# Buffers of one SBUF and PSUM slot each, chosen by the kernel's own planner

## The chip, the core and the metric

The program runs on one core of a Trainium2 chip. The metric is the device time of one execution in microseconds (us); less is better. The core has a matrix engine (TensorE, PE in the profile, with its weight loads as PEld), a vector engine (DVE), a scalar engine (ACT), a general engine (POOL, hardly used here), and a sync engine (SP), whose queue issues every DMA of this kernel.

## The reference

Three layers follow each other: an attention over 32 memory slots for each of 8 batches and 8 heads (576 tokens each), then two feed-forward layers over the 4608 tokens, all in float32.

```python
a = softmax(phi)                                  # over the 32 slots
k_m, v_m = einsum('bhsm,bhsd->bhmd', a, k), einsum('bhsm,bhsd->bhmd', a, v)
attn = softmax(q @ k_m.T / sqrt(64));  x = attn @ v_m       # [4608, 512]
x = (s * relu(x @ w_in) ** 2 + b) @ w_out                   # 512 -> 2048 -> 512
x = gelu_sigmoid(x @ w1) @ w2                               # 512 -> 2048 -> 512
```

## The kernel before, in words

Each float32 operand of a large product is split into a high and a low part (`hi`, `lo`, with tiles named oh and ol, or ah and al, mh and ml for the first product), and each product is three matmuls: high by high, high by low, low by high. The second to fourth products are cut in 2 by 2 blocks and use seven block products in place of eight (three forms of Strassen's scheme), which is why blocks are subtracted from each other (`minus`, `half`) ahead of the split. Products accumulate in PSUM in tiles named X, Y and Z, and while one of them is being added up, its state is copied out several times (tiles a, u2, u4 and c12, called a, u and c in the profile).

The time falls in four stages. Until about 300 us runs the attention with the first product (its results h are rectified and stored to DRAM as r). Then `down("wo")` runs until about 650 us, `up` (to the tiles g, a and ab, stored to DRAM) until about 1000 us, and `last` until the end. Between stages the data goes through DRAM, so every stage loads its blocks by DMA (A, B, C, D, E, x) and stores its results by DMA. All of these share one in-order queue on SP.

The order of the work isn't written out by hand. The methods of `Net` hand operations to an `Order`: each has a due time, one or more engines with a cost, and the tiles that it reads and writes. `Order.sort` then plans: it goes through the operations that are ready, reckons for each when it could start (its engine's time, the ends of what it reads, and a slot for each new tile), and takes one after the other. The list that comes out is the order in which instructions are issued, engine by engine; nothing reorders an engine later.

Slots: `BUFS` gives the number of buffers of each tag: 31 of tag t (nearly every block, operand and result), 30 of tag w (weights), 4 of tag ps (PSUM), and a few small ones. The planner keeps a heap `free[tag]` of the reckoned times at which slots come free. An operation that makes a new tile starts no earlier than the smallest of them; when the operation is taken, that time is popped. When the last user of a tile has been planned, the reckoned end of its last use plus 0.2 us is pushed. A DMA's reckoned end is its start plus its KB over 340 plus 3.0 us. The heap holds times alone, so the planner doesn't say which slot a tile gets.

That is settled by the framework. `Net.t` asks a pool for a tile with `tag=k[0]` and `bufs=` the number of `BUFS`. The framework gives the new tile one of the tag's slots and makes the first instruction that writes it wait until every instruction that used the slot's former tile has ended. If that is on another engine or a DMA, the wait is a semaphore wait, and what is queued behind the waiting instruction on its engine waits as well.

Lines of the profile that the prediction uses: L1049 to L1051 are the matmuls of `up` into X or Y, L1118 to L1120 those into Z in `phase`, L1182 to L1184 those of `last` and L1284 to L1286 its Z; L1061 is ScalarE's copy of X into u2 or u4, L266 and L267 the high part, L272 a subtraction, the low part or an addition on VectorE, L815 the rectified h, L261 the DMA. The planner's own lines in the diff are in `Order.sort`, and the pool's call is in `Net.t`.

Of the kernel before, what the change touches and what calls it, by code (L numbers as in the profile page):

```python
# [27 lines left out]
class Order:  # L28
# [14 lines left out]
    def __init__(self, bufs):  # L43
        self.bufs, self.ops, self.rank, self.fill, self.until, self.since = bufs, [], [], None, 0, 0
        self.narrow = set()
        self.wrote, self.read, self.users = {}, {}, {}

    def add(self, due, ways, r=(), w=(), first=0):
# [19 lines left out]
    def sort(self):  # L68
        ops, rank = self.ops, self.rank
        left = [len(o[2]) for o in ops]  # L70
        after = [[] for _ in ops]
        tiles = {}
        for n, (due, _, deps, new) in enumerate(ops):
            for d in deps:
                after[d].append(n)
            for x in new:
                tiles.setdefault(x[0], []).append((due, n, x))
        queue = {tag: [x for _, _, x in sorted(v, key=lambda e: e[:2])] for tag, v in tiles.items()}
        free = {tag: [0.0] * n for tag, n in self.bufs.items()}
        uses = {x: len(v) for x, v in self.users.items()}  # L80
        last = dict.fromkeys(uses, 0.0)
        at, end, on, out = {}, [0.0] * len(ops), [None] * len(ops), []
        of = [[] for _ in ops]
        for x, v in self.users.items():
            for n in v:
                of[n].append(x)
        run = False
        held = {"dve": 0.0, "pool": 0.0}
        ready = sorted((rank[n], n) for n in range(len(ops)) if not left[n])
        since = {n: 0.0 for _, n in ready}  # L90
        while ready:
            can = {}
            limit = ready[0][0] + self.AHEAD
            for due, n in ready:
                if due > limit and can:
                    break
                _, ways, deps, new = ops[n]
                t0 = 0.0
                if new:
                    ok = True  # L100
                    for tag in {x[0] for x in new}:
                        mine = [x for x in new if x[0] == tag]
                        f = free[tag]
                        if len(f) < len(mine) or any(x not in queue[tag][:len(f)] for x in mine):
                            ok = False
                            break
                        t0 = max(t0, f[0] if len(mine) == 1 else heapq.nsmallest(len(mine), f)[-1])
                    if not ok:
                        continue
                best = None  # L110
                for i, (eng, cost, _, port) in enumerate(ways):
                    t = max(t0, at.get(eng, 0.0))
                    if port:
                        t = max(t, held["dve" if eng == "pool" else "pool"])
                    for d in deps:
                        e = end[d] + (self.LAG[eng] if on[d] != eng else 0.05)
                        if e > t:
                            t = e
                    score = t + cost * self.WEIGHT.get(eng, 1.0)
                    if best is None or score < best[0]:  # L120
                        best = score, t, eng, i
                can.setdefault(best[2], []).append((best[1], due, n, best[3]))
            if not can:
                raise RuntimeError("no order")
            first = []
            for tag, v in can.items():
                t0 = min(v)[0]
                like = [c for c in v if c[0] <= t0 + 0.1 and c[2] in self.narrow and c[1] >= self.since] if tag == "pe" and run else ()
                if like:
                    c = min(like, key=lambda c: c[1:])  # L130
                    if c[1] < min(v, key=lambda c: c[1:])[1] + self.NEAR:
                        first.append(c)
                        continue
                first.append(min((c for c in v if c[0] <= t0 + (self.SLACK if c[1] < self.until else 0.0)), key=lambda c: c[1:]))
            t, _, n, i = min(first)
            _, ways, _, new = ops[n]
            eng, cost, fn, port = ways[i]
            if port:
                held[eng] = t + cost
            if self.fill and eng == "pe":  # L140
                out.append(lambda n=int((t - at.get(eng, 0.0)) * self.FILL): self.fill and self.fill(n))
            for x in new:
                queue[x[0]].remove(x)
                heapq.heappop(free[x[0]])
            at[eng], on[n] = t + cost, eng
            end[n] = t + cost + (3.0 if eng == "sync" else 0.0)
            ready.remove((rank[n], n))
            if eng == "pe":
                run = n in self.narrow
            out.append(fn)  # L150
            for m in after[n]:
                left[m] -= 1
                if not left[m]:
                    bisect.insort(ready, (rank[m], m))
            for x in of[n]:
                last[x] = max(last[x], end[n])
                uses[x] -= 1
                if not uses[x]:
                    heapq.heappush(free[x[0]], last[x] + 0.2)
        self.span = max(end)  # L160
        self.end, self.on = end, on
        return out


class Net:
# [50 lines left out]
    def t(self, k, shape, dt=F32):  # L216

        self.n += 1
        pool = self.ps if k[0] == "ps" else self.sb
        x = pool.tile(shape, dt, tag=k[0], bufs=self.BUFS[k[0]], name=f"{self.name(k)}_{self.n}")  # L220
        self.T[k] = x
        return x

# [1255 lines left out]
```

## Time and profile before

| | us |
|---|---|
| median of 3 runs | 1352.02 (1351.92 to 1352.36) |
| the profiled execution, whole | 1353.97 |
| its span, from the first to the last instruction | 1352.2 |
| TensorE busy | 1335.0 |
| VectorE busy | 1103.3 |
| ScalarE busy | 843.2 |

The profiled execution's whole time is 1.8 us above its span and 1.95 us above the median of the runs that were timed without a profile. Matmuls overlap and their ends are modelled, so how often a matmul starts says more than the busy time does. The granted clock of TensorE was full (a mean of 0.997) except in the first slices of the span.

### The profile page before, as it was taken

The numbers are of one execution on the slowest core, as the hardware profiler recorded it, in microseconds if no ns is written. First come the engines' busy times: TensorE is split into PE (matmuls) and PEld (weight loads), VectorE is DVE, ScalarE is ACT, GpSimd is POOL, SyncE is SP. The second block draws the span as 40 slices with busy tenths as digits, with TensorE's granted clock in tenths as the row PEclk, the third lists the DMA queues.
The fourth block names the chain that finished last, engine by engine and source line by source line (L and its number), as shares of the span: only waits on it lengthen the run. The fifth ranks groups of instructions, "written<-read, shape, count | busy, mean of one in ns | idle before, by whom it ended". The sixth has DMA issues, their size and how long they took to land.

```text
span 1352.2 us, 24079 instructions
## 1 busy us (share of the span) xinstructions
PE 1335.0 (99%) x9112; PEld 1293.7 (96%) x9112; DVE 1103.3 (82%) x1568; ACT 843.2 (62%) x1164; POOL 52.2 (4%) x42
## 2 busy tenths in 40 slices
PE   6999999999999999999999999999999999999998
PEld 5888888899999999999999999999999999999998
DVE  6878996899998897999875778594376988889796
ACT  4766666788877887787654655564455454355452
POOL 2201220200000000000000000000000000000000
PEclk8999999999999999999999999999999999999999
DMA  9989999797755685499989699978998765747563
GB/s 364 352 299 353 361 344 329 259 325 261 280 190 168 221 318 164 180 318 332 375 326 369 243 340 333 319 263 302 382 333 305 242 207 180 257 140 240 173 207 121
DMA packets 141091, 374.37 MB, mean 277 GB/s; under 512 B 15920, under 2 KB 18480, under 8 KB 140976
## 3 DMA queue, kind: packets, MB, share of 16 engines
q1 hardware_dynamic: 140976, 372.85, 78.5%
q8 instruction: 71, 1.16, 0.4%
q14 instruction: 44, 0.36, 0.1%
HBM read 235.10 MB, written 137.69 MB: 276 GB/s over the span
## 4 chain that ended last, share of the span: by engine, by line
PE 92%; DVE 4%; DMA 3%; issue 0%; ACT 0%; SPq 0%; ACTq 0%
PE X L1184 5%; PE X L1183 5%; PE X L1182 5%; PE X L1049 5%; PE X L1051 5%; PE X L1050 5%; PE X L909 5%; PE X L911 5%; PE X L910 5%; PE h L296 4%; PE h L298 4%; PE h L297 4%; PE Y L910 2%; PE Y L1184 2%; PE Y L911 2%; PE Y L1182 2%
## 5 line engine op out<-in xcount | busy, mean ns | idle before, releaser
L296 PE MATMUL h<-ah,mh 128*128 128x288 f32 x512 | 155.1, 303 | 0.2
L298 PE MATMUL h<-ah,ml 128*128 128x288 f32 x512 | 151.3, 295 | 0.1
L297 PE MATMUL h<-al,mh 128*128 128x288 f32 x512 | 150.8, 295 | 0.0
L1049 PE MATMUL X<-oh,w 128*128 128x384 f32 x384 | 128.6, 335 | 1.1 <-ACT u L1061 1.1
L911 PE MATMUL X<-oh,wo 128*128 128x384 f32 x384 | 128.4, 334 | 0.0
L910 PE MATMUL X<-ol,wo 128*128 128x384 f32 x384 | 128.4, 334 | 0.0
L909 PE MATMUL X<-oh,wo 128*128 128x384 f32 x384 | 128.3, 334 | 0.0
L1050 PE MATMUL X<-ol,w 128*128 128x384 f32 x384 | 128.3, 334 | 0.0
L1051 PE MATMUL X<-oh,w 128*128 128x384 f32 x384 | 128.3, 334 | 0.0
L1183 PE MATMUL X<-ol,w 128*128 128x384 f32 x384 | 128.3, 334 | 0.0
L1182 PE MATMUL X<-oh,w 128*128 128x384 f32 x384 | 128.3, 334 | 0.0
L1184 PE MATMUL X<-oh,w 128*128 128x384 f32 x384 | 128.3, 334 | 0.0
L815 ACT ACTIVATE r<-h 128x576 f32<-128x576 f32 x126 | 88.7, 705 | 61.7 <-PE h L298 45.9
L296 PEld LDWEIGHTS h<-ah,mh 128*128 128x128 f32 x512 | 96.1, 188 | 13.7 <-issue 6.6
L272 DVE TENSOR_TENSOR u<-Y,u 128x768 f32<-128x768 f32 (+1 forms) x62 | 57.5, 928 | 51.4 <-PE Y L1051 34.1
L266 ACT CAST oh<-C 128x768 fp32r<-128x768 f32 x82 | 70.8, 872 | 45.4 <-PE X L910 11.6
L272 DVE TENSOR_TENSOR ol<-A,oh 128x768 fp32r<-128x768 f32 x96 | 88.7, 953 | 12.1 <-issue 3.7
L298 PEld LDWEIGHTS h<-ah,ml 128*128 128x128 f32 x512 | 96.1, 188 | 0.5 <-DVE ml L272 0.4
L297 PEld LDWEIGHTS h<-al,mh 128*128 128x128 f32 x512 | 96.2, 188 | 0.0
L272 DVE TENSOR_TENSOR ol<-C,oh 128x768 fp32r<-128x768 f32 x84 | 79.4, 955 | 17.9 <-PE X L911 3.4
L266 ACT CAST oh<-A 128x768 fp32r<-128x768 f32 x91 | 77.0, 867 | 16.8 <-DVE ol L272 5.1
L1049 PEld LDWEIGHTS X<-oh,w 128*128 128x128 f32 x384 | 72.1, 188 | 1.8 <-ACT u L1061 1.8
(269 smaller groups left out, 3710.5 us busy)
## 6 DMA issues: line engine op xcount, KB each, us to landing
w<-w SPq DMA_DIRECT2D x120, 512.0 KB, 6.2
r<-r SPq DMA_DIRECT2D x128, 288.0 KB, 4.3
kv<-in_kv SPq DMA_DIRECT2D x72, 258.0 KB, 5.1
g<-u SPq DMA_DIRECT2D x48, 384.0 KB, 4.5
raw<-in_w SPq DMA_DIRECT2D x32, 512.0 KB, 5.9
q<-in_q SPq DMA_DIRECT2D x32, 288.0 KB, 5.6
A<-r SPq DMA_DIRECT2D x24, 384.0 KB, 5.0
B<-r SPq DMA_DIRECT2D x24, 384.0 KB, 5.1
```

Of the source, the lines that this page charges most:

```text
L272: self.order.add(due, [self.dve(n, lambda: nc.vector.tensor_tensor(out(), a(), b(), op=op), port=port)], r, w, first)
L296: self.nc.tensor.matmul(ps, wh, xh, start=start and i == 0, stop=False)
L297: self.nc.tensor.matmul(ps, wh, xl, start=False, stop=False)
L298: self.nc.tensor.matmul(ps, wl, xh, start=False, stop=(i == n - 1))
L909: nc.tensor.matmul(out, T[w][:, 0, c], T[h][:, p], start=f, stop=False, skip_group_check=True)
L910: nc.tensor.matmul(out, T[w][:, 0, c], T[l][:, p], start=False, stop=False, skip_group_check=True)
L911: nc.tensor.matmul(out, T[w][:, 1, c], T[h][:, p], start=False, stop=last, skip_group_check=True)
L1049: nc.tensor.matmul(out, T[w][:, 0, c], T[h][:, k], start=f, stop=False, skip_group_check=True)
L1050: nc.tensor.matmul(out, T[w][:, 0, c], T[l][:, k], start=False, stop=False, skip_group_check=True)
L1051: nc.tensor.matmul(out, T[w][:, 1, c], T[h][:, k], start=False, stop=k == 1, skip_group_check=True)
L1182: nc.tensor.matmul(out, T[w][:, 0, c], T[h][:, p], start=f, stop=False, skip_group_check=True)
L1184: nc.tensor.matmul(out, T[w][:, 1, c], T[h][:, p], start=False, stop=last, skip_group_check=True)
```

## The change

The heap of free slots holds pairs of a reckoned time and a slot's number in place of times. The slot that is popped for a new tile is kept in `Order.slot`, and goes back to the heap with the reckoned time at which the tile's last use ends. `Net.t` asks the pool for a tile of a tag that has the slot's number in it (t0, t1, and so on), with one buffer. So the framework has nothing to choose: the tile waits for the former tile of that slot. The reckoned times are the same pairs' first parts, so the planned order of the operations, their engines and the number of slots stay as they were.

```diff
-        free = {tag: [0.0] * n for tag, n in self.bufs.items()}
+        free = {tag: [(0.0, i) for i in range(n)] for tag, n in self.bufs.items()}
...
-                        t0 = max(t0, f[0] if len(mine) == 1 else heapq.nsmallest(len(mine), f)[-1])
+                        t0 = max(t0, f[0][0] if len(mine) == 1 else heapq.nsmallest(len(mine), f)[-1][0])
...
             for x in new:
                 queue[x[0]].remove(x)
-                heapq.heappop(free[x[0]])
+                self.slot[x] = heapq.heappop(free[x[0]])[1]
...
                 if not uses[x]:
-                    heapq.heappush(free[x[0]], last[x] + 0.2)
+                    heapq.heappush(free[x[0]], (last[x] + 0.2, self.slot[x]))
...
-        x = pool.tile(shape, dt, tag=k[0], bufs=self.BUFS[k[0]], name=f"{self.name(k)}_{self.n}")
+        x = pool.tile(shape, dt, tag=f"{k[0]}{self.order.slot[k[:2]]}", bufs=1, name=f"{self.name(k)}_{self.n}")
```

## Rows read from the trace of the kernel before

**Rows 1.** The page, part 1: each engine's busy us, share, instructions.

```profile
PE 1335.0 (99%) x9112; PEld 1293.7 (96%) x9112; DVE 1103.3 (82%) x1568; ACT 843.2 (62%) x1164; POOL 52.2 (4%) x42
```

**Rows 2.** Windows: stretch, its length, each engine's busy us, clock, DMA share, GB/s.

```profile
0.00:62.00 62.00, 50.42 (x514) 41.59 (x522) 47.27 (x78) 37.11 (x61) 15.80 (x16) 0.94 0.96 358
62.00:300.00 238.00, 237.66 (x2550) 206.49 (x2535) 202.65 (x318) 164.49 (x247) 36.42 (x26) 1.00 0.93 324
300.00:650.00 350.00, 349.92 (x2041) 349.57 (x2040) 316.11 (x410) 281.73 (x383) 0.00 (x0) 1.00 0.73 248
650.00:1000.00 350.00, 348.86 (x2012) 348.17 (x2011) 241.84 (x394) 191.89 (x261) 0.00 (x0) 1.00 0.89 323
1000.00:1352.00 352.00, 348.19 (x2009) 347.87 (x2007) 295.44 (x371) 167.98 (x216) 0.00 (x0) 1.00 0.63 214
```

**Rows 3.** The chain that ended last, whole span: start us, us, what.

```profile
861.25 7.36 DMA g<-u
...
1348.23 0.56 DVE u L272
```

**Rows 4.** Waits of TensorE, whole span: us in total, times, longest us.

```profile
PE s L578 <- DMA kv<-in_kv: 4.6, 2, 3.0
...
PE X L1049 <- ACT u L1061: 1.1, 2, 0.7
```

**Rows 5.** Timeline, 868 to 870: start us, us, engine, line, what, idle before.

```profile
868.62 0.34 PE L1119 MATMUL Z<-ol,w 128*128 128x384 f32 x1
...
868.70 0.80 ACT L1061 COPY u<-X 128x768 f32<-128x768 f32 x1 [5.86 <-DMA g<-u]
868.79 0.34 PE L1120 MATMUL Z<-oh,w 128*128 128x384 f32 x1
869.16 0.33 SPq L261 DMA_DIRECT2D x<-x  x1
...
869.55 0.44 PE L1049 MATMUL X<-oh,w 128*128 128x384 f32 x1 [0.43 <-ACT u L1061]
```

**Rows 6.** Timeline, 975 to 986, of SP, TensorE and ScalarE.

```profile
975.27 0.32 SPq L261 DMA_DIRECT2D g<-ab  x1
...
981.81 0.33 PE L1051 MATMUL X<-oh,w 128*128 128x384 f32 x1
...
983.89 0.34 PE L1120 MATMUL Z<-oh,w 128*128 128x384 f32 x1
...
984.09 0.80 ACT L1061 COPY u<-X 128x768 f32<-128x768 f32 x1 [5.88 <-PE Z L1119]
984.26 0.79 SPq L261 DMA_DIRECT2D A<-g  x2
...
984.94 0.44 PE L1049 MATMUL X<-oh,w 128*128 128x384 f32 x1 [0.71 <-ACT u L1061]
```

**Rows 7.** DMAs of 968 to 986, and of the whole span: KB, us to landing.

```profile
g<-ab SPq DMA_DIRECT2D x1, 384.0 KB, 3.6
...
g<-u SPq DMA_DIRECT2D x48, 384.0 KB, 4.5
```

**Rows 8.** Timeline of TensorE, 75 to 77.

```profile
75.80 0.29 PE L297 MATMUL h<-al,mh 128*128 128x288 f32 x1
76.24 0.40 PE L298 MATMUL h<-ah,ml 128*128 128x288 f32 x1
```

**Rows 9.** Waits of ScalarE and VectorE in 1000 to 1352, of SP throughout.

```profile
ACT oh L266 <- PE X L1183: 25.1, 17, 3.9
...
DVE ol L272 <- PE X L1183: 19.8, 16, 3.2
...
SPq L261 <- PE X L911: 83.5, 41, 10.2
```

**Rows 10.** Timeline, 1201 to 1204: an operand's low part and its first reader.

```profile
1201.95 0.96 DVE L272 TENSOR_TENSOR ol<-rb,oh 128x768 fp32r<-128x768 f32 x1
...
1203.64 0.33 PE L1285 MATMUL Z<-ol,we 128*128 128x384 f32 x1
```

More of the change, by code (lines that the diff above doesn't have):

```diff
@@ L45, in __init__ @@
         self.narrow = set()
+        self.slot = {}
         self.wrote, self.read, self.users = {}, {}, {}
```

## The prediction
> **What bounds the kernel now.** The first view to read is the share of each engine: TensorE is busy for 1335.0 of 1352.2 us, VectorE for 1103.3, ScalarE for 843.2 [rows 1]. A mean over four stages can hide a stage with another limit, so the second view is the busy time by stretch [rows 2]. Its length less TensorE's busy time is 11.58 us in the first 62 us, then 0.34, 0.08, 1.14 and, in the last stretch, 3.81 us. The last of these is the tail: the last sum on VectorE starts at 1348.23 and a store follows [rows 3]. So from 62 us to the tail TensorE stands still for some 1.6 us in all, and is the bound in each of the four stages. In no stage is VectorE as busy: 316 of 350 us is its most.
>
> The third view, who ended TensorE's waits, says what there is to win [rows 4]. The long ones lie in the first 62 us and are waits for data, the loads of k and v first (4.6 us). After 62 us one line alone is left, the matmuls of X in the third stage that wait for ScalarE's copy of X, 1.1 us in two waits.
>
> Busy time hides short stops, since a matmul of 334 ns starts every 173 ns. The spacing of starts is finer: 868.62 to 868.79 is the regular pace [rows 5]. I went through the spacings of all matmuls after 62 us and found six places where it is broken by more than the pattern of its stage. Two are the copies above. The first of the others is in [rows 8]: 75.80 to 76.24 in place of 0.13 us, and the late matmul itself takes 0.40 instead of 0.29. The other three, near 108, 245 and 381 us, are of the same kind and a little smaller; all four wait for a low part from VectorE.
>
> **What the change touches.** The order of the instructions on each engine, their number and their costs stay. What moves is which older tile each new tile has to wait for. So the terms are the waits that end with a slot, and the question is which of them reach TensorE.
>
> **The wait at 984.** ScalarE copies X into u at 984.09, after 5.88 us of idle time that ended with a matmul of Z (L1119) [rows 6]. That matmul has nothing to do with X: it read the tile that held the slot before. The copy runs 0.80 us, and TensorE, which goes on in X only when the copy is done, starts its next matmul at 984.94. By the pace it would have started at 983.89 + 0.17 = 984.06, so 0.88 us are lost, and that matmul takes 0.44 instead of 0.34, another 0.10: 0.98 us. Was another slot free? The store of ab was issued at 975.27 and a store there took 3.6 us to land [rows 6, 7], so the slot of ab was free at about 978.9; it lay idle for almost 6 us and went to the second load of the pair that starts at 984.26. The planner reckons a store of 384 KB at 384/340 + 3.0 + 0.2 = 4.3 us, so it reckons this slot free near 979.6, well ahead of one that matmuls still read at 984. With the change the copy takes the slot of ab. Its data is ready when the last matmul of X ends, at 981.81 + 0.33 = 982.14 [rows 6], 1.9 us ahead of 984.06, and the 0.80 us fit in. Term: -0.98 us. The load that had the slot of ab now waits for the matmul, some 5 us at 979 to 984 or not at all; it stood behind the load at 984.26 in SP's queue anyway, which itself waited until then, so nothing is lost by it.
>
> **The wait at 868.** The same copy waits 5.86 us for the store of u, which took 7.36 us instead of the usual 4.5 [rows 3, 5, 7]. TensorE loses 869.55 - 868.79 - 0.17 = 0.59 and 0.10 in the matmul after it, 0.7 us. Here I see no slot that lay idle: the load at 869.16 and the high part right after it start with the end of a matmul of Z as well. Another choice can't make a slot free that isn't, so I keep this wait: 0, with -0.70 as the one end, if the copy is given the slot of something that ends a little earlier, and +0.70 as the other, if one more copy falls on a late store.
>
> **The four small stops.** By the spacings they cost (0.44 - 0.13) + (0.40 - 0.29) = 0.42 us at 75 us [rows 8] and some 0.36 at each of the other three, 1.5 us in all. They end with VectorE's own queue, which is full there, not with a slot. Term: 0, with -1.5 as the far end.
>
> **The start.** In the first 40 us each tile gets a slot that nothing has used; the old heap and the new one both hand these out first. After that the slots have been free for long. TensorE's waits there are for data [rows 4], with the same queues before and after. Term: 0.
>
> **Waits off TensorE.** ScalarE's high parts in the last stage wait 25.1 us for one line of matmuls, VectorE's low parts 19.8 us, and SP's loads 83.5 us for a line of the second stage [rows 9]. None of these instructions reads PSUM; all are waits for a slot, and behind each stands its whole queue. They cost nothing at present, because operands are made well ahead of their matmuls. The shortest lead that I found in the last stage is a low part that ends at 1202.91 and is read at 1203.64, 0.73 us [rows 10]. That is the cover, and it sets what is given back: if TensorE comes 0.98 us earlier and VectorE doesn't, it waits there for 0.98 - 0.73 = 0.25 us. VectorE's queue waits for slots that TensorE frees, so it comes earlier too, in part. Term: between 0 and +0.25; I take +0.1.
>
> **Sum.** -0.98 + 0.1 = -0.9 us of the profiled span of 1352.2. The tail and what lies around the span aren't touched, so the median moves by as much: 1352.02 - 0.9 = 1351.1 us. With the far ends of the terms it could be -0.98 - 0.70 - 1.5 = -3.2, which is 1348.8.
>
> **Rival 1: nothing, or all of it given back.** The framework's own choice may be as good as the planner's nearly everywhere. For it: TensorE has no more than two waits for slots in some 1290 us. And the waits of [rows 9] recur all through a stage, on the line that frees the oldest operands, as they would if all slots were in use and none lay idle. Then 984 is one accident that the new choice trades for another, and the time is 1352.0, with 0.5 us to either side. Against it: the idle slot at 984 is in the rows.
>
> The Trainium skill's "Perfetto Trace Analysis", section Optimization Strategy, says that a gap that repeats on the engine that should be saturated can mean that there isn't enough SBUF or PSUM for the next tile. By that, choosing among slots adds none, and the time would be that of this rival. The trace agrees for ScalarE and VectorE [rows 9] and not for TensorE, where nothing repeats [rows 4].
>
> **Rival 2: more than that.** If the small stops go as well, as slot waits ahead of VectorE's queue shorten, the time goes to 1348.8 to 1349.3. Against it: they don't end with a slot.
>
> **Rival 3: slower.** The new choice trusts the planner's times. A store is reckoned at 4.3 us for 384 KB; the median of the stores of u is 4.5, and one took 7.36 [rows 3, 7]. A slot behind such a store is reckoned free up to 3 us too early, and whoever is given it waits with its queue. The place where this counts is the copy of X in the third stage: the two breaks show that the copy and its wait have about one microsecond of cover before TensorE stops. The stage has 24 passes with three copies each, 72 copies; if one in ten is given a slot that is a late store's, that is 7 times the 0.70 us of 868, 4.9 us less the gain of 0.98: 1356. It decides from the fifth such copy on: 5 x 0.70 - 0.98 = 2.5 us. For it: DMA engines are busy for 0.89 of the third stage [rows 2], where landings scatter. Against it: the two breaks are all there is in 72 copies, under a choice that doesn't know of stores either; and the planner's caution of 4.3 us is close to the median.
>
> **How the numbers follow.** 0.2% of the time, 2.7 us, is about what a measurement of this kernel can tell from no change. The forecast, 1350.3 to 1351.6, has 0.56; rival 1, 1351.5 to 1352.5, has 0.27; rival 2 has 0.06; rival 3, 1354 to 1358, has 0.11. The forecast and rival 1 both lie within 0.2%, and so does a half of rival 2 and a little of rival 3. So faster by over 0.2% (under 1349.3) has 0.05, within 0.2% has 0.85, slower (over 1354.7) has 0.10. The range leaves out the far half of rival 2 and the upper part of rival 3: 1349.2 to 1354.2.
>
> **What would show it.** In the profile of the changed kernel, TensorE's waits after 62 us no longer have a copy that waits for a matmul of Z; the copy near 984 runs right after the matmuls of X, before Z ends. The wait for the store of u near 868 is there again or has moved. TensorE's busy time by stretch is 348.9 to 349.9 in the third, and the start's 50.4 us are as before. The waits of ScalarE and VectorE for matmuls in the last stage change by no more than a few microseconds. I am wrong if TensorE's waits have new lines for copies of X or for operands in the third or last stage (rival 3), if the first 62 us change, since nothing here explains that, or if an engine has another number of instructions that do work.

## The result, and the profile after

The changed kernel takes 1360.67 us (1360.43 to 1362.46) beside 1352.01 us for the kernel before in the same comparison: a ratio of 1.0066, 95% interval 1.0053 to 1.0078. The forecast was 1351.1 us and the range ended at 1354.2, so the result is slower than all that was reckoned with. Line numbers of the changed kernel are one higher than before.

The first two views are the shares of the engines and the windows by stage; columns as in [rows 1, 2].

```profile
PE 1346.6 (99%) x9112; PEld 1305.4 (96%) x9112; DVE 1105.3 (81%) x1568; ACT 843.6 (62%) x1164; POOL 52.3 (4%) x42
```

```profile
0.00:62.00 62.00, 54.06 (x548) 43.54 (x549) 49.14 (x82) 37.74 (x62) 15.81 (x16) 0.94 0.97 368
62.00:300.00 238.00, 237.86 (x2523) 208.01 (x2523) 204.94 (x317) 166.90 (x249) 36.45 (x26) 1.00 0.93 324
300.00:650.00 350.00, 350.00 (x2023) 349.51 (x2022) 313.01 (x406) 277.83 (x378) 0.00 (x0) 1.00 0.73 246
650.00:1000.00 350.00, 350.00 (x2001) 350.00 (x2000) 240.48 (x392) 192.12 (x261) 0.00 (x0) 1.00 0.88 319
1000.00:1358.00 358.00, 354.71 (x2026) 354.39 (x2024) 297.77 (x374) 169.03 (x217) 0.00 (x0) 1.00 0.63 214
```

The number of working instructions is that of before, the granted clock is the same, and TensorE doesn't stand still from 300 to 1000 us. All the same it starts fewer matmuls there: 2023 against 2041, and 2001 against 2012 in a stretch in which the kernel before even had two stops [rows 2]. The engine that sets the time is never idle and yet slower.

TensorE's waits (columns as in [rows 4]) no longer have a copy of X among them, and none of these rows lies after 62 us:

```profile
PE s L579 <- DMA kv<-in_kv: 3.0, 2, 1.5
PE vw L794 <- ACT mh L267: 1.9, 1, 1.9
PE warm L235 <- POOL ident masks.py:199: 1.4, 1, 1.4
PE x L666 <- ACT km L267: 0.6, 1, 0.6
PE y L684 <- DVE st L704: 0.5, 1, 0.5
PE a L671 <- ACT sc L693: 0.3, 1, 0.3
```

So the aim was reached and the time got worse. Where the time went stands in the groups by line (line, engine, names, shapes, count | busy us, mean ns of one | idle before). First a line of the kernel before, then the same line and one of the last stage in the changed kernel:

```profile
L909 PE MATMUL X<-oh,wo 128*128 128x384 f32 x384 | 128.3, 334 | 0.0
```

```profile
L910 PE MATMUL X<-oh,wo 128*128 128x384 f32 x384 | 129.7, 338 | 0.0
L1183 PE MATMUL X<-oh,w 128*128 128x384 f32 x384 | 129.6, 338 | 0.0
```

Each matmul takes 1% longer, in all three feed-forward stages. A timeline shows it at single starts (start us, us, engine, line, what):

```profile
700.01 0.34 PE L1050 MATMUL Y<-oh,w 128*128 128x384 f32 x1
700.19 0.34 PE L1051 MATMUL Y<-ol,w 128*128 128x384 f32 x1
700.37 0.34 PE L1052 MATMUL Y<-oh,w 128*128 128x384 f32 x1
700.55 0.34 PE L1050 MATMUL Y<-oh,w 128*128 128x384 f32 x1
```

The starts lie 0.18 us apart where 868.62 to 868.79 was 0.17 [rows 5]. Taken over all 384-column matmuls from 1000 to 1345 us, the mean distance of starts is 173.33 ns before and 175.15 after. From 300 us on, some 5,900 such distances at 175.07 - 173.35 = 1.72 ns more make 10.1 us. That is more than the whole loss of 8.66, so about 1.5 us should have been gained elsewhere.

What differs on TensorE, if neither order, shape nor clock does? The addresses. With one tag for 30 or 31 buffers, the framework lays the buffers of a tag side by side. With a tag for each buffer it lays them out in the order of their first use, so that slots of w (4096 bytes in each partition), of t (3072) and of the small groups (8 to 1024 bytes) are mixed through SBUF, and the small ones shift what follows. The addresses in the two programs:

```
remainder of a slot's first byte by 256:    0   32   64   96  128  160  224
before, w slots                             -    -    -    -    -    -   30
before, t slots                             -    -    -    -    -    -   31
after,  w slots                             7    6    2    -    3    6    6
after,  t slots                             8    3    1    -    1   13    5
```

### The profile page after: what moved, and what is told of

The parts are those of the page before. It is cut to its first block, busy times and chain, and to the rows that moved or that the text cites. A ratio compares the mean times of both kernels' runs of the same rounds, so it can differ in the third digit from the quotient of the medians.

```text
span 1358.3 us, 24048 instructions
## 1 busy us (share of the span) xinstructions
PE 1346.6 (99%) x9112; PEld 1305.4 (96%) x9112; DVE 1105.3 (81%) x1568; ACT 843.6 (62%) x1164; POOL 52.3 (4%) x42
## 4 chain that ended last, share of the span: by engine, by line
PE 95%; DMA 3%; DVE 2%; SPq 0%; issue 0%; ACT 0%
PE X L910 5%; PE X L1052 5%; PE X L1050 5%; PE X L1183 5%; PE X L1185 5%; PE X L1184 5%; PE X L911 5%; PE X L1051 5%; PE X L912 5%; PE h L297 5%; PE h L299 4%; PE h L298 4%; PE Y L911 2%; PE Y L1184 2%; PE Y L1183 2%; PE Y L1185 2%
## 5 line engine op out<-in xcount | busy, mean ns | idle before, releaser
L273 DVE TENSOR_TENSOR u<-Y,u 128x768 f32<-128x768 f32 (+1 forms) x62 | 57.5, 929 | 53.8 <-PE Y L1052 37.6
L910 PEld LDWEIGHTS X<-oh,wo 128*128 128x128 f32 x384 | 72.2, 188 | 0.2 <-ACT u L957 0.2
```

The source lines that it names most:

```text
L273: self.order.add(due, [self.dve(n, lambda: nc.vector.tensor_tensor(out(), a(), b(), op=op), port=port)], r, w, first)
L910: nc.tensor.matmul(out, T[w][:, 0, c], T[h][:, p], start=f, stop=False, skip_group_check=True)
```

## The experiments

Two theories at first. "Place": the slots' new addresses slow the matmuls. "Choice": which tile follows which in a slot slows them. The remainders in the texts written ahead are by 128, which is where the suspicion began; that the pattern repeats by 256 came out of the runs. "Pace" below is the mean distance of starts of the 384-column matmuls from 1000 to 1345 us.

**Choice and place crossed.** One kernel keeps the new choice and gives each group a pool of its own, which puts the addresses back:

```diff
+        self.group = {g: ctx.enter_context(tc.tile_pool(name=f"sb_{g}", bufs=1)) for g in self.BUFS if g != "ps"}
...
-        pool = self.ps if k[0] == "ps" else self.sb
+        pool = self.ps if k[0] == "ps" else self.group[k[0]]
```

> The changed kernel with its choice of slots left as it is, but with a pool of its own for each group, so that the 30 slots of w lie side by side again, then the 31 of t, then the small ones, all at the addresses that they have in the kernel before. Theory 'place' (the matmuls of the feed-forward stages start 175.1 ns apart and not 173.35 because w and t slots are mixed through SBUF): spacing 173.3 to 173.5 ns, and the gains of the start and of the small stops stay: 1348 to 1350 us. Theory 'choice' (it is the tile that stands in a slot, and the order in which slots come round, that slows the matmuls): spacing 175 ns, 1359 to 1361 us.

Measured: 1350.55 us (1350.03 to 1351.68), ratio 0.9989 (0.9980 to 0.9999), pace 173.33 ns: the pace of "place", and a time 0.55 us above the range written for it.

The other takes each tile's slot from a list of those that the kernel before gives it, and leaves them at the changed kernel's addresses:

```diff
-        x = pool.tile(shape, dt, tag=f"{k[0]}{self.order.slot[k[:2]]}", bufs=1, name=f"{self.name(k)}_{self.n}")
+        x = pool.tile(shape, dt, tag=f"{k[0]}{self.SLOTS[self.n - 1]}", bufs=1, name=f"{self.name(k)}_{self.n}")
```

> The other half of the cross: each tile in the slot that it has in the kernel before (from a list), but the slots laid out as in the changed kernel, w, t and small ones mixed in the order of first use. Theory 'place': spacing 175 ns, and without the gains of the start and the stops 1361 to 1364 us. Theory 'choice': 173.4 ns and 1351.5 to 1352.5 us.

Measured: 1362.92 us (1362.83 to 1363.96), ratio 1.0081 (1.0066 to 1.0096), pace 175.23 ns. So the place alone costs 10.8 us, the choice alone gains 1.5, and together they make 9.3 where 8.66 was measured. "Choice" has fallen. The windows show both (250 us of the third and of the last stage: length, TensorE's busy us and matmuls, clock, DMA share, GB/s); the kernel with the old choice in the new place:

```profile
700.00:950.00 250.00, 250.00 (x1429) 1.00 0.85 307
1010.00:1260.00 250.00, 250.00 (x1429) 1.00 0.67 231
```

and the one with the groups apart:

```profile
700.00:950.00 250.00, 250.00 (x1444) 1.00 0.87 314
1010.00:1260.00 250.00, 250.00 (x1445) 1.00 0.65 222
```

15 matmuls fewer in 1444 are 1.0%.

**Mixed order or mixed remainders?** The small groups alone get a pool behind the rest. The slots of w and t stay mixed, but every slot of both has the remainder of before.

```diff
+        self.small = ctx.enter_context(tc.tile_pool(name="sb_small", bufs=1))
...
-        pool = self.ps if k[0] == "ps" else self.sb
+        pool = self.ps if k[0] == "ps" else self.sb if k[0] in ("w", "t") else self.small
```

> The changed kernel with the small groups alone in a pool of their own behind the rest: w and t slots stay mixed in the order of first use, but each begins at 96 bytes above a multiple of 128, as in the kernel before (in the changed one they begin at 0, 32, 64 or 96). Within theory 'place': if the mixing of w and t costs the pace, 175 ns and 1359 to 1361 us; if it is the remainder of the address, 173.4 ns and 1348 to 1350 us. Theory 'choice': 1359 to 1361 us.

Measured: 1350.30 us (1349.54 to 1352.65), ratio 0.9988 (0.9979 to 0.9998), pace 173.33 ns. That w and t are mixed costs nothing; it is the remainders.

**Is one remainder bad?** Three kernels shift all slots of the kernel before by 32, 64 and 96 bytes:

```diff
+        self.gap = self.sb.tile([P, 8], F32, name="gap")
+        nc.vector.memset(self.gap, 0.0)
```

(16 and 24 in place of 8 for the other two.)

> The kernel before with one unused tile of 32 bytes ahead of the slots (and one memset on VectorE that fills it), so that every slot of w and t begins at a multiple of 128 and not 96 above one; choice, order and neighbours are unchanged. If the remainder of the address sets the pace: 175 ns or more and 1358 to 1364 us, or, if 0 is the better remainder, below 1351 us. If it is the mixing, or the choice: 1351.7 to 1352.6 us.

> The kernel before with an unused tile of 64 bytes ahead of the slots: all slots of w and t begin at 32 above a multiple of 128 (the commonest remainder in the changed kernel). If some remainders are slow by themselves (32 or 64): spacing of the 384-column matmuls about 175 ns, 1360 us or more. If it is only the mixture of remainders: 173.3 ns, 1351.5 to 1353 us, as with 0.

> The same with 96 bytes: all slots of w and t at 64 above a multiple of 128. If some remainders are slow by themselves: about 175 ns, 1360 us or more. If it is only the mixture: 173.3 ns, 1351.5 to 1353 us.

Measured: 1352.71 us with a ratio of 1.000 (0.999 to 1.001), 1352.26 and 1352.25 (one run each, beside 1352.97 for the kernel before), pace 173.33 in all three. No remainder is bad as long as all slots share it.

**What must agree?** Every w slot at 96 by 128 (224 by 256) and every t slot at 0, with the new choice and a pool for each group. From here to the last experiment each kernel was run once:

```diff
+        self.group = {g: ctx.enter_context(tc.tile_pool(name=f"sb_{g}", bufs=1)) for g in ("w", "gap", "t", "km", "an", "nm", "sm")}
...
+        self.gap = self.group["gap"].tile([P, 8], F32, name="gap")
+        nc.vector.memset(self.gap, 0.0)
```

> The changed kernel with a pool for each group (as in the run with groups apart), and 32 unused bytes between the slots of w and those of t: every w slot at a remainder of 96, every t slot at 0. If a mixture of any kind costs the pace (what TensorE reads as operands against what it reads as weights): 175 ns, 1358 to 1361 us. If it costs only where the slots of one group differ: 173.3 ns, 1349.5 to 1351 us.

Measured: 1369.18 us, pace 176.58 ns. That is more than either expectation, and nearly twice the loss of the changed kernel. Its windows:

```profile
700.00:950.00 250.00, 250.00 (x1418) 1.00 0.85 307
1010.00:1260.00 250.00, 250.00 (x1418) 1.00 0.68 230
```

Then half of the slots of both groups moved on, by 32, by 128 and by 64 bytes; the small groups are apart.

```diff
+        if k[0] in ("w", "t"):
+            self.seen.add((k[0], self.order.slot[k[:2]]))
+            if len(self.seen) == 31 and not self.gap:
+                self.gap = self.sb.tile([P, 8], F32, name="gap")
+                self.nc.vector.memset(self.gap, 0.0)
```

(32 and 16 in place of 8 for the other two.)

> The changed kernel with the small groups apart, and 32 unused bytes after the first 30 slots of w and t: those 30 at a remainder of 96, the other 31 at 0, both of which are quick where all slots have them. If the mixture within a group costs the pace: 175 ns, 1358 to 1361 us. If only the remainders 32 and 64 do: 173.3 ns, 1349.5 to 1351 us.

> As the run with half of the slots 32 bytes on, but with 128 unused bytes after the first 30 slots of w and t: all remainders by 128 agree (96), those by 256 and more don't. If only the remainder by 128 counts (or by 64 or less): 173.3 ns, 1349.5 to 1351 us. If a larger one does: 174.5 ns or more, 1356 to 1360 us.

> The same with 64 unused bytes: all remainders by 64 agree (32), those by 128 don't (96 and 32). If only the remainder by 64 counts: 173.3 ns, 1349.5 to 1351 us. If that by 128 does: 174.5 ns, 1356 to 1360 us.

Measured: 1357.80, 1361.11 and 1356.54 us; pace 174.50, 175.21 and 174.30. All three cost, the one with 128 the most and a little more than was expected at the most, so slots that agree by 128 may still disagree. With the groups the other way round (w at 0, t at 96; the unused tiles are 32 bytes ahead of w and 96 between w and t):

```diff
+        self.fit = self.group["fit"].tile([P, 8], F32, name="fit")
+        nc.vector.memset(self.fit, 0.0)
+        self.gap = self.group["gap"].tile([P, 24], F32, name="gap")
+        nc.vector.memset(self.gap, 0.0)
```

> The changed kernel with a pool for each group and the remainders the other way round: every w slot at 0, every t slot at 96. If a difference between weights and operands costs the same either way: 176.5 ns, 1367 to 1370 us, as with w at 96 and t at 0. If its sign matters (in the run with half the slots 32 bytes on, long stretches with weights at 0 and operands at 96 ran at 173 to 174 ns): 173.3 to 174 ns, 1350 to 1354 us.

Measured: 1369.18 us, pace 176.58 ns. The second of the two expectations, drawn from stretches of the run with 32 bytes, was wrong: by 256, those stretches have operands at 224 and this run has them at 96, and the table further down gives 173.33 ns for the one and 176.67 for the other.

**TensorE by itself.** Is it TensorE's own reads that have to agree, or its reads and what other engines and DMAs write? All of the network is left out; one line of matmuls for each stretch:

```diff
+    for out_, w_, m_, first, last in block([(0, 96, 96)]): mm(out_, w_, m_, start=first, stop=last, skip_group_check=True)
```

The three numbers are the remainders of weights, high operand and low operand.

> Nothing of the network is computed: TensorE multiplies fixed tiles, with the order of operands of the feed-forward stages (weights high, high operand; same weights, low operand; weights low, high operand), 128x384, in 24 stretches of 288 matmuls (about 50 us each), and no DMA or other engine works beside it but in the last two. Stretches 1 to 16: weights at remainder 0, operands at 0, 32, 64 ... 480. 17: both at 96. 18: weights 96, operands 0. 19: weights 0, operands 96. 20: every 12 matmuls all at 96, then all at 0. 21: weights 0, high operand 0, low operand 96. 22: weights 96, operands 0 and 96 in turn every 12. 23 and 24: all at 0, while VectorE copies 128x512 at remainder 0, then at 96. Theory 'operands' (it is what TensorE itself reads that must agree): 173.3 ns in 1, 17 and 23 to 24, 176.5 ns in 18, 174 to 176 ns in 20 to 22. Theory 'traffic' (the disagreement matters between TensorE's reads and what other engines and the DMA write): 173.3 ns in 1 to 22, and 175 ns or more in 24.

Mean distance of starts over each stretch after its first 100 matmuls, worked out from the starts in the trace:

```
weights 0, operands at       0      32      64      96     128     160     192     224
ns                      173.33  173.33  173.34  176.68  176.02  173.33  174.66  173.33
operands at                256     288     320     352     384     416     448     480
ns                      173.34  173.34  173.33  176.67  176.03  173.33  174.66  173.34
all at 96  173.34 | weights 96, operands 0  176.65 | weights 0, operands 96  176.65
every 12 all at 96, then all at 0  173.86 | weights and high 0, low 96  176.67
weights 96, operands 0 and 96 in turn  175.26 | all 0, VectorE at 0  173.33 | at 96  173.34
```

The windows say the same in counts: stretches 4 and 6 (operands at 96 and at 160), then the last two, in which the third pair of columns is VectorE's.

```profile
162.00:210.00 48.00, 48.00 (x274) 48.00 (x273) 0.00 (x0) 0.00 (x0) 1.00 0.00 1
265.00:313.00 48.00, 48.00 (x279) 48.00 (x278) 0.00 (x0) 0.00 (x0) 1.00 0.00 1
```

```profile
1119.00:1167.00 48.00, 48.00 (x279) 48.00 (x278) 37.71 (x89) 0.00 (x0) 1.00 0.00 1
1169.00:1217.00 48.00, 48.00 (x279) 48.00 (x278) 37.64 (x89) 0.00 (x0) 1.00 0.00 1
```

TensorE alone, from the second stretch on with no DMA and no other engine at work, shows the whole effect, and VectorE's 89 copies beside it add nothing. "Operands" holds and "traffic" falls, though in stretches 20 and 21 the figures lie 0.1 and 0.7 ns outside what was written for them. The pattern repeats every 256 bytes, and three of the eight remainders cost: 96, 128 and 192.

The Trainium skill's "SBUF — State Buffer", section "SBUF: two separate sides", says that TensorE, ScalarE and VectorE's own pair of ports never wait on anyone. The last two stretches agree for VectorE beside TensorE (173.33 and 173.34 ns).

**All pairs, and one of them put into the kernel.**

```diff
+    for wr in range(0, 256, 32):
+        for mr in range(0, 256, 32):
+            for out_, w_, m_, first, last in block([(wr, mr, mr)]): mm(out_, w_, m_, start=first, stop=last, skip_group_check=True)
```

> TensorE alone again, nothing of the network computed: 64 stretches of 96 matmuls of 128x384, weights at each of the remainders 0, 32 ... 224 by 256 bytes, operands (high and low alike) at each of the eight. If the pace depends on the difference alone, every row is the first one turned (operand behind weights by 0, 32, 64, 160, 224: 173.3; 96: 176.7; 128: 176.0; 192: 174.7 ns). But the stretch with weights at 96 and operands at 0 (behind by 160) has already taken 176.66, so a table that isn't of the difference alone is expected: about half of the pairs at 173.3 and the rest at 174.5 to 176.7. If the table explains the changed kernel, its mean over the pairs that stand there comes to about 175 ns, and for the runs with half of the slots moved on to 174.3 to 175.2.

The mean distance of starts from the 24th matmul of each stretch on, worked out from the starts in the trace:

```
ns       operands   0      32      64      96     128     160     192     224
weights   0    173.33  173.33  173.33  176.67  175.94  173.33  174.65  173.33
weights  32    173.33  173.33  173.33  173.33  176.67  175.93  173.33  174.64
weights  64    176.67  173.33  173.33  173.33  173.33  176.67  175.93  173.33
weights  96    173.33  174.64  173.33  173.33  173.33  173.33  176.67  175.94
weights 128    175.93  173.33  174.64  173.33  173.32  173.33  173.33  176.67
weights 160    176.67  176.07  176.67  174.71  173.33  173.33  173.33  173.33
weights 192    173.33  176.67  175.93  173.33  174.64  173.33  173.33  173.33
weights 224    176.67  173.33  176.67  175.94  173.33  174.64  173.32  173.33
```

Mostly the rows are the first one turned, so the difference of the two remainders decides: operands 96, 128 or 192 bytes behind the weights (by 256) cost 3.3, 2.6 or 1.3 ns. Three pairs (weights, operands) depart from that by 2 ns or more: (64, 0), (160, 64) and (224, 0). And the pair (96, 0) ran at 173.33 here and at 176.65 in the first run of TensorE alone, so one pair can run at either pace.

The kernel with half of the slots 32 bytes on shows that within one execution. By the starts in its trace and the addresses in its program, it has 49 stretches of 12 or more matmuls with the pair (224, 0) after 300 us. Past their first seven distances, 30 of them run at 173 to 174 ns and 19 at 176.5 to 177.4. What came before counts: 13 of the 14 that follow matmuls of the pair (0, 0) are slow, and 2 of the 18 that follow (224, 224). Why is open.

The kernel with w at 0 and t at 64 differs from the one of 1369.18 us by 32 bytes:

```diff
-        self.gap = self.group["gap"].tile([P, 24], F32, name="gap")
+        self.gap = self.group["gap"].tile([P, 16], F32, name="gap")
```

> The changed kernel with a pool for each group, every w slot at a multiple of 256 and every t slot at 64 above one: the groups differ by 64, in place of 96 in the run that took 1369.18 us. By the stretches of TensorE alone (weights 0, operands 64: 173.34 ns against 176.66 for 96): 173.3 to 173.5 ns, 1349.5 to 1352 us. If any difference between the groups costs the pace in the kernel: 176 ns, 1364 us or more.

Measured: 1350.39 us (the kernel before: 1352.14), pace 173.51 ns. Its windows:

```profile
700.00:950.00 250.00, 250.00 (x1442) 1.00 0.86 312
1010.00:1260.00 250.00, 250.00 (x1443) 1.00 0.65 220
```

Two groups at different remainders are nearly free if their pair is a free one. The two runs of 1369.18 us fit too: by 256 their pairs are (224, 0) and (0, 96), 176.67 ns each in the table. So the table holds in the kernel as well, where a pair stays the same.

Does it explain the changed kernel? The mean of the table over the pairs that stand there is 174.44, 1.1 ns of the 1.74 above 173.33; about 175 had been expected. For the half of slots moved by 32, 128 and 64 the table gives 174.19, 174.63 and 173.65, below the paces by 0.3 to 0.7.

What the table leaves out is the change from one pair to another, and the traces price it. In the run of all pairs the same kind of change costs the same each time: from operands 224 bytes behind the weights to both at one remainder, the first distances are 173, 173, 175, 177, 185, 176 and 182 ns (weights at 32; the same to 1 ns at the others), some 28 ns more than the pace, and then 173 to 174. From both at one remainder to operands 32 behind costs nothing. All of these pairs are free by the table. The stretch with a change every 12 matmuls lost 0.53 ns a matmul. In the changed kernel from 300 to 1345 us, the operand's remainder by 256 differs from one matmul to the next in some 3,290 of 5,890 cases. The 0.6 ns that the table leaves are then 1.1 ns for each of them. That the changes are all of the rest is an estimate from these figures, not measured by itself.

**The gain of the choice.** The kernel with the small groups apart, once more:

> The changed kernel with the small groups apart, once more, for the size of what the choice alone gives: by the prediction's steps 1350.3 to 1351.6 us (ratio 0.9987 to 0.9997); by the first run of it 1350.3 (0.9979 to 0.9998). If the choice gives nothing that can be told from noise, the interval holds 1.

Measured: 1350.28 us (1349.78 to 1351.28), ratio 0.9987 (0.9978 to 0.9996). This version beats both kernels, the one before by 0.1% and clear of noise: the change together with a pool that keeps the small tiles from shifting the large ones.

## Why the prediction was wrong

The step that failed is the first sentence on what the change touches: "the order of the instructions on each engine, their number and their costs stay". The order and the number did. The cost of a matmul didn't: the 384-column ones start 175.07 ns apart and not 173.35, some 10 us in all, because a tag for each buffer also changes where buffers lie. I read the diff as a choice among slots and didn't ask how the framework lays out 61 large slots once they have tags of their own. No row of the kernel before could have priced it: there all slots share one remainder. But the question could have been asked, and then the cost of 5,900 matmuls stood open: 1 ns on each is 5.9 us, six times the one term that I worked out.

Point by point:

- **The wait at 984** (term -0.98): right, and by the step that was given. The distances at this place sum to 0.98 or 0.99 us more than the pace in the five kernels with the old choice (before, the three shifts, and the old choice in the new place), and to 0.02 or less in the ten with the new one. In the program before, the slot of this copy had held an operand that matmuls of Z read; in the changed program it had held ab, whose store was the last to use it. In the kernel shifted by 32 bytes, whose line numbers are two higher than before, the copy still waits for the matmul of Z:

```profile
982.94 0.80 ACT L1063 COPY u<-X 128x768 f32<-128x768 f32 x1 [5.88 <-PE Z L1121]
983.79 0.44 PE L1051 MATMUL X<-oh,w 128*128 128x384 f32 x1 [0.71 <-ACT u L1063]
```

- **The wait at 868** (0, with 0.70 to both sides): gone, but not by the change. It is gone in the three shifted kernels as well, so it belonged to the one profiled execution, with its store of 7.36 us [rows 3]. The choice didn't touch it: in both programs the copy's slot held the u that is being stored. In the changed kernel the same copy, the 30th of 48, follows right on the matmuls of X:

```profile
870.43 0.80 ACT L1062 COPY u<-X 128x768 f32<-128x768 f32 x1 [4.37 <-PE X L1052]
```

- **The four small stops** (0, far end -1.5): wrong for two. Those near 108 and 245 us are there in the same five kernels and gone in the same ten, where matmuls follow each other by 0.13 us; they make 0.36 us each, 0.7 in all. "They end with VectorE's own queue, not with a slot" was an argument from who ended the wait alone. The matmul that waits doesn't read the low part ml. It writes a tile h, and in the program before this h has the PSUM slot of a vw that VectorE still reads to make an ml. Near 245 us that is the first of the two ml in the row below, which ends at 245.02. In the changed program h has the slot of an older h, and the matmul starts at 243.09, while the first ml still runs (until 243.29). The stop near 108 is alike. Before, then in the changed kernel:

```profile
243.80 2.35 DVE L272 TENSOR_TENSOR ml<-vw,mh 128x1024 fp32r<-128x1024 f32 x2
245.07 0.40 PE L296 MATMUL h<-ah,mh 128*128 128x288 f32 x1
```

```profile
242.08 2.35 DVE L273 TENSOR_TENSOR ml<-vw,mh 128x1024 fp32r<-128x1024 f32 x2
243.09 0.30 PE L297 MATMUL h<-ah,mh 128*128 128x288 f32 x1
```

  So these were waits for a slot, a PSUM slot on TensorE itself, and rival 2 was right about two of the four stops, though not about how. The stops near 75 and 381 us, where the matmul does read a low part, are still there in the changed kernel.
- **The start** (0): not settled. The first 62 us did change, which the prediction named as a sign of being wrong: TensorE is busy for 54.06 us of them in place of 50.42. One and the same matmul started at 57.46 us before and at 55.70 after. But it started at 57.01 in the kernel shifted by 32 bytes and at 56.32 in the one shifted by 64, where nothing else was changed. The wait for k and v, 4.6 us before [rows 4], is 3.0 in the changed kernel and in the one shifted by 32 bytes too:

```profile
PE s L580 <- DMA kv<-in_kv: 3.0, 2, 1.5
```

  The start scatters by a microsecond between these kernels, and one profile of each can't tell a gain of that size from it: that matmul lies at 56.3 to 57.5 us in the five kernels with the old choice and at 55.5 to 56.6 in the ten with the new.
- **Waits off TensorE** (+0.1): ScalarE's wait for that line of matmuls is 23.2 us in place of 25.1 and VectorE's 11.0 in place of 19.8 [rows 9], the second more than the few microseconds that were said. In the third and the last stage TensorE waits nowhere for an operand, so nothing was given back.

```profile
ACT oh L267 <- PE X L1184: 23.2, 17, 2.4
DVE ol L273 <- PE X L1184: 11.0, 10, 3.3
```

- **Sum**: -0.9 us for the choice. The waits that went with it are 0.98 + 0.72 = 1.7 us. With the addresses held, the choice measures 1350.28 to 1350.55 us beside 1352.09 and 1352.14, that is -1.5 to -1.9, at the lower edge of the forecast's own case (1350.3 to 1351.6). So for the choice the mechanism was right and the term of the small stops, put at 0, was too small by 0.7. The 10 us that came on top were in none of the cases: rival 3 ended on the slow side, but by late stores, and TensorE's waits show none.

## What to carry to other kernels

Before a change to tags, pools or tile sizes is priced, write down the addresses that tiles will get, by the remainder of 256 bytes, since a kernel bound by TensorE pays for each matmul that reads at an unlucky distance. Keep the slots of weights and operands at one remainder, and give small tiles a pool of their own behind the large ones. And when the bound engine is never idle and yet slower, look at the mean of one instruction and at the distance of starts, not at the waits.

## What was not expected of the hardware

- The distance of starts of 128x384 float32 matmuls depends on where weights and operands lie in SBUF relative to each other. With TensorE alone at work and weights at 0, the pattern repeats every 256 bytes: 173.33 ns at five of eight differences, 174.65, 175.94 and 176.67 at the others. Three of the 64 pairs depart from the rule of the difference by 2 ns or more.
- A matmul's own pair isn't all that counts. In the kernel with half of the slots 32 bytes on, matmuls whose neighbours on both sides all read at one remainder still start 174.8 ns apart, not 173.33. Where the seven matmuls before read there too, it is 173.34, and so it is with 128 and 64 bytes (173.35 and 173.34): a change of remainder is paid for over some seven matmuls. Some pairs can run at either of two paces, which what came before them decides in part. Why is open.
- A pair that stays the same is steady: with w at 96 and t at 0 (by 128) the pace is 176.56 ns in the third stage and 176.58 in the last, and 1369.18 us came out for both orders of the groups.
